# Running all six key chunks' scores of pairs 10 and 11 as one TensorE group

## The chip, the core and the metric

The kernel runs on one core of one Trainium2 chip. The core has a TensorE (PE: matmuls; PEld: the loading of its stationary operand), a VectorE (DVE), a ScalarE (ACT), a GpSimd (POOL) and a SyncE (SP), which run side by side and wait for one another by semaphores; DMA engines move data. The metric is device time in microseconds (us) for one execution; lower is better.

## What is computed

The reference joins a sparse attention and a mixture of experts. Cut to what matters:

```python
# attention: q, k, v are (4 batches, 8 heads, 768 tokens, 64)
k_sum = k.reshape(B, H, 24, 32, D).max(axis=3)      # one summary key for each 32 tokens
v_sum = v.reshape(B, H, 24, 32, D).mean(axis=3)
scores_l = scale * q @ k.T, kept where |i - j| < 16   # local band
scores_s = scale * q @ k_sum.T + log(32)             # summaries
a = softmax(concat(scores_l, scores_s)); attn = a @ concat(v, v_sum)
# experts: x is attn as (3072 tokens, 512)
P = sinkhorn(exp(x @ w_gate))                        # 8 rounds of row and column scaling
out = sum over e of P[:, e] * (relu(x @ w1[e]) @ w2[e])   # 8 experts, hidden size 1024
```

## The kernel before

**Pairs.** Attention is done for pairs of heads: 4 batches x 8 heads give 16 pairs, 0 to 15, four for each batch. A pair has two heads of 64 channels, which lie in partitions 0 to 63 and 64 to 127, and six chunks of 128 tokens. Pairs 0 to 3 are done in halves of three chunks by functions of their own (names ending in `_h`); pairs 4 to 15 go through `pair_start` and `pair_whole`.

**Steps of one pair (4 to 15).** Keys and queries come by GpSimd's DMA (`load_qk`, L284) and are transposed to kT and qT: for pairs below `BY_DMA` = 12 on TensorE (L303) with a copy out (L207), for 12 to 15 by DMA transposes on SyncE's queue (`tr_dma`, L330). VectorE takes the maximum over 32 keys (`key_max`, L335) and splits it by head (L341). TensorE multiplies keys and queries in the band, 64 rows by 128 columns (L347, tile sg). ScalarE exponentiates (`score_exp`, L408, tile er), VectorE multiplies by the band (`masks`, L412, tile em) and by the band's edges (`edges`, L420 and L424, tile Ee). TensorE multiplies queries by the summary keys (L461, tile ss), ScalarE exponentiates (L472). Values: block sums on TensorE (L357, tile vs), out by VectorE (L363, L367), the neighbours' values by small DMAs (`near_values`, L377 and L379; on SyncE's queue for pairs below 12, on GpSimd's from 12). TensorE multiplies by the values (L435, L441, tile av), VectorE normalizes (L542, L543, tile xs), and the result is transposed into xT, on TensorE (L550) with a copy or, for pairs 12 to 14, by DMA (L560).

**Halves or whole.** The scores of a pair need 2 heads x 6 chunks of 160 columns. A half (three chunks, both heads) fills the two PSUM banks of tag "s". For pairs below `WHOLE` the first half (`scores`) is exponentiated by one activation of 128x960; the second half (`scores_1`) takes the same two banks after that, and again one activation of 128x960. From `WHOLE` on, `scores` runs all six chunks in one go: the second half goes to two banks of tag "a", of which there are three, shared with transposes, block sums, summaries, values and logits, and is exponentiated by two activations of 128x480, one for each head.

**Experts.** Expert 0 (L211 to hidden tiles hps, L216 to outputs yps, in three banks of tag "m") runs on the tokens as they become ready, between the steps of attention. When a batch is ready its logits are taken (L570). Experts 1 to 7 follow (L764, L786, L798, L815, L830, L839, L843) with the Sinkhorn rounds (L579 to L593) among the first of them.

**Order.** The program isn't scheduled by the compiler. `Plan` (L34 to L125) is a list scheduler that runs while the kernel is built: each step is added with its engine (or a choice of ScalarE and VectorE), a cost, its dependencies, a priority and the PSUM buffers that it opens or uses; `order` picks the step that can start first and writes out one fixed order for each engine. Costs of the steps at hand: scores of a half 0.4, of a whole 0.6, exponentials 0.97 and 0.53 us. So an edit to one step can move many others, on every engine, and can change which of ScalarE and VectorE takes a step. Each engine then works through its order and waits where a semaphore isn't there yet. SyncE's transposes for a pair (L889) also wait for the scores of the pair three before.

Of the kernel before, what the change touches and what calls it, by code (L numbers as in the profile page):

```python
# [33 lines left out]
class Plan:  # L34
# [7 lines left out]
    def add(self, eng, cost, fn, deps=(), prio=0.0, opens=(), uses=(), lag=0.0):  # L42
        u = Unit(eng, cost, fn, [d for d in deps if d is not None], prio, list(opens), lag)
        for b in list(opens) + list(uses):
            b.users.append(u)
        if uses and eng != "PE":
            u.prio -= 100.0
        self.units.append(u)
        return u
# [79 lines left out]
def kernel(  # L129
# [29 lines left out]
    NEH = 3  # L159
    BY_DMA = 12  # L160
    X_BY_DMA = 12
    WHOLE = 12
    FILL = {"v0": 1, "S0": 1, "s0": 2, "s1": 1, "s2": 1}

    const = ctx.enter_context(tc.tile_pool(name="const", bufs=1))
# [60 lines left out]
    with tc.manual_schedule():  # L226
# [35 lines left out]
        def bank(tag, name, dtype=FP32):  # L262
            pool, n = (mps, 3) if tag == "m" else (aps, NA)
            return pool.tile([128, 2048 // mybir.dt.size(dtype)], dtype, tag=tag, name=name, bufs=n)
# [117 lines left out]
        def scores(i):  # L382
            sg = at["sg", i, 0] = banks2("sg")
            dst = [[sg[:, j, :] for j in range(2)], None]
            if i >= WHOLE:
                dst[1] = at["sg", i, 1] = [bank("a", "sg1") for _ in range(2)]
            score_mms(i, dst, range(G if i >= WHOLE else HG))

# [4 lines left out]
        def score_mms(i, dst, chunks):  # L393
            for g in chunks:
                for j in range(2):
                    o = (g % HG) * LIVE
                    score_mm(i, dst[g // HG][j][:, o:o + LIVE], j, g, 0, LIVE)

        def score_exp(i, h, j=None):
            if h == 0:  # L400
                at["er", i] = attn.tile([128, 2, G, LIVE], BF16, tag="er", name="er", bufs=2)
                at["em", i] = attn.tile([128, 2, G, 128], BF16, tag="em", name="em", bufs=2)
            er, sg = at["er", i][:, :, HG * h:HG * (h + 1), :], at["sg", i, h]
            if j is None:
                dst, src = er.rearrange("p j g l -> p j (g l)"), sg[:, :, 0:HG * LIVE]
            else:
                dst, src = er[:, j].rearrange("p g l -> p (g l)"), sg[j][:, 0:HG * LIVE]
            nc.scalar.activation(out=dst, in_=src, func=AF.Exp, bias=0.0, scale=SCALE)  # L408
# [535 lines left out]
        def pair_whole(i, prio):  # L944
# [3 lines left out]
            deps = [U["kT", i, 0], U["kT", i, 1], U.get(("ed", i - 2))]  # L948
            bufs = [Buffer("s")] + (2 * [None] if i < WHOLE else [Buffer("a"), Buffer("a")])
            U["S", i, 0] = U["S", i, 1] = add("PE", 0.4 if i < WHOLE else 0.6, lambda: scores(i), deps, prio,  # L950
                                              opens=[x for x in bufs if x is not None])
            U["X", i, 0] = add("ACT", 0.97, lambda: score_exp(i, 0), [U["S", i, 0]], prio, uses=bufs[:1])
            if i < WHOLE:
                buf = Buffer("s")
# [366 lines left out]
```

The softmax here doesn't subtract the row's maximum and nothing guards it: scores larger than these inputs give would overflow.

## Time and profile before

| | |
|---|---|
| median of 5 runs | 667.11 us (666.8 to 670.0) |
| the profiled execution | 668.27 us, its span 666.4 us |
| mean granted TensorE clock | 0.997 |
| TensorE busy | 658.5 us |
| first half of pair 10's scores starts at | 70.12 us |
| last score matmul (pair 15) starts at | 108.0 us |
| exponentials of scores | 20 of 128x960 and 8 of 128x480 |

A line of the timeline gives the start, the time from the first start to the last end, engine, line, operation, what is written and read, and how many in a row. Matmuls are pipelined and overlap, so the distance between starts tells what a group takes of TensorE. A line of waits gives engine and waiting line, who ended the wait, the sum of us, how many times, and the longest.

### The profile page before, as it was taken

Reading aid. Unit: us, or ns where it says so; the run is one execution under the profiler, and the core shown is the slowest. Engines: PE = TensorE matmul, PEld = TensorE weight load, DVE = VectorE, ACT = ScalarE, POOL = GpSimd, SP = SyncE. Lnnn points to the kernel's source line nnn. Section 1 sums busy time; section 2 is a strip of 40 time slices with the busy share of each in tenths; the row PEclk is TensorE's granted clock in tenths of the full one; section 3 lists DMA queues with packets and bytes.
Section 4 is the critical chain, followed back from the end, with each engine's and each line's share of the span. In section 5 each row is a group of like instructions: output and inputs, shape, how many; then the busy total and the mean of one; then the engine's idle time right before and its main releaser. Section 6 shows DMA issues by size and latency. Waiting matters only on the chain.

```text
span 666.4 us, 13247 instructions
## 1 busy us (share of the span) xinstructions
PE 658.5 (99%) x5132; PEld 436.7 (66%) x5132; DVE 550.3 (83%) x1034; ACT 411.9 (62%) x769; POOL 198.8 (30%) x257
## 2 busy tenths in 40 slices
PE   8999999999999999999999999999999999999997
PEld 4666666555676666666666666666666666666666
DVE  6899977798989787888789887888778877988776
ACT  5667876556876566556565665656565656556652
POOL 8899622100132222222221222222122213222123
PEclk8999999999999999999999999999999999999999
DMA  9999982700763747473654756373837465334656
GB/s 169 168 147 144 134 85 42 128 0 1 127 115 65 123 71 121 79 127 64 95 102 72 127 81 108 68 127 62 130 64 127 77 99 96 64 63 110 155 136 202
DMA packets 112558, 67.89 MB, mean 102 GB/s; under 512 B 77936, under 2 KB 90480, under 8 KB 112496
## 3 DMA queue, kind: packets, MB, share of 16 engines
q0 software_dynamic: 94816, 57.46, 65.1%
q1 hardware_dynamic: 17152, 9.58, 6.5%
q8 instruction: 40, 0.66, 0.4%
q14 instruction: 22, 0.18, 0.1%
q10 hardware_dynamic: 528, 0.02, 0.0%
HBM read 52.45 MB, written 6.29 MB: 88 GB/s over the span
## 4 chain that ended last, share of the span: by engine, by line
PE 96%; DVE 2%; DMA 1%; issue 0%; ACT 0%; POOLq 0%; DVEq 0%
PE yps L815 22%; PE pA L764 22%; PE pY L815 17%; PE pQ L764 11%; PE hps L211 6%; PE yps L216 6%; PE pR L764 5%; PE sg L347 1%; DMA qst<-in_q_dram 1%; PE av L512 1%; PE vs L357 1%; PE tkq L303 1%; PE av L435 1%; DVE xs L543 1%; PE ss L461 1%; PE av L441 1%
## 5 line engine op out<-in xcount | busy, mean ns | idle before, releaser
L815 PEld LDWEIGHTS <-h 128*128 128x128 f16 x2352 | 230.1, 98 | 89.2 <-issue 1.3
L843 POOL DMA_DIRECT2D out_acc<-y x120 | 101.4, 888 | 372.4 <-ACT y L839 106.4
L839 ACT ACTIVATE y<-pY,P_sb 128x256 f32<-128x256 f32 x168 | 80.0, 477 | 126.1 <-PE pY L815 124.6
L830 DVE SCALAR_TENSOR_TENSOR out_acc<-yps,P_sb,out_acc 128x512 f32<-128x512 f32 x128 | 95.1, 744 | 28.0 <-PE yps L815 27.9
L798 DVE TENSOR_TENSOR h<-h 128x1024 f16<-128x1024 f16 x168 | 109.1, 684 | 1.3
L815 PE MATMUL pY<-w,h 128*128 128x256 f16 x672 | 100.3, 273 | 0.6 <-ACT y L839 0.6
L764 PE MATMUL pA<-xT,w 128*128 128x512 f16 x336 | 98.6, 379 | 0.0
L815 PE MATMUL yps<-w2sum,h 128*128 128x256 f16 x672 | 97.9, 273 | 0.0
L815 PE MATMUL yps<-w,h 128*128 128x256 f16 x672 | 93.3, 273 | 0.0
L830 DVE SCALAR_TENSOR_TENSOR out_acc<-pY,P_sb,out_acc 128x512 f32<-128x512 f32 x84 | 62.8, 748 | 29.1 <-PE pY L815 27.6
L764 PEld LDWEIGHTS <-w 128*128 128x128 f16 x672 | 65.8, 98 | 31.3 <-issue 0.2
L764 PEld LDWEIGHTS <-w1sum 128*128 128x128 f16 x504 | 49.3, 98 | 44.7
L786 DVE CUSTOM_DVE_ANT_0 h<-pQ,snap 128x512 f16<-128x512 f32 x84 | 57.6, 686 | 6.5 <-ACT snap L207 3.6
L786 DVE CUSTOM_DVE_ANT_0 h<-pA,snap 128x512 f16<-128x512 f32 x84 | 57.3, 683 | 5.4 <-PE pA L764 5.1
L202 ACT ACTIVATE h<-pA 128x512 f16<-128x512 f32 x84 | 50.7, 603 | 12.1 <-PE pA L764 12.0
L202 ACT ACTIVATE h<-pR 128x512 f16<-128x512 f32 x84 | 50.1, 596 | 8.1 <-PE pR L764 8.1
L207 ACT COPY pR<-pA 128x512 f32<-128x512 f32 x82 | 46.8, 571 | 6.7 <-PE pA L764 5.9
L815 PE MATMUL pY<-w2sum,h 128*128 128x256 f16 x336 | 50.4, 273 | 0.1
L764 PE MATMUL pA<-xsum,w 128*128 128x512 f16 x168 | 50.0, 379 | 0.0
L764 PE MATMUL pQ<-xsum,w1sum 128*128 128x512 f16 x168 | 50.0, 379 | 0.0
L764 PE MATMUL pR<-xT,w 128*128 128x512 f16 x168 | 50.0, 379 | 0.0
L764 PE MATMUL pQ<-xT,w1sum 128*128 128x512 f16 x168 | 50.0, 379 | 0.0
(150 smaller groups left out, 856.7 us busy)
## 6 DMA issues: line engine op xcount, KB each, us to landing
out_acc<-y POOLq DMA_DIRECT2D x120, 256.0 KB, 3.4
w<-in_moe_w_dram POOLq DMA_DIRECT2D x14, 1024.0 KB, 10.3
out_dram<-out_acc SPq DMA_DIRECT2D x24, 256.0 KB, 2.4
qst<-in_q_dram POOLq DMA_DIRECT2D x32, 96.0 KB, 5.6
vx<-in_v_dram POOLq DMA_DIRECT2D x15, 192.0 KB, 6.4
kst<-in_k_dram POOLq DMA_DIRECT2D x24, 96.0 KB, 5.9
w<-in_moe_w_dram POOLq DMA_DIRECT2D x4, 256.0 KB, 8.0
w<-in_moe_w_dram POOLq DMA_DIRECT2D x2, 512.0 KB, 8.3
```

What stands on the lines that cost most here:

```text
L202: nc.scalar.activation(out=out, in_=in_, func=AF.Relu, bias=0.0, scale=1.0)
L207: (nc.scalar.copy if eng == "ACT" else nc.vector.tensor_copy)(out=out, in_=in_)
L211: nc.tensor.matmul(hp[:, 0:n], lhsT=w1s[e][:, dk, f * 128:(f + 1) * 128], rhs=xT[:, dk, t0:t0 + n], start=(dk == 0), stop=(dk == KD - 1))
L216: nc.tensor.matmul(yp[:, d], lhsT=h[:, f, c * 128:(c + 1) * 128], rhs=w2s[e][:, f, d], start=(f == 0), stop=(f == KF - 1))
L303: nc.tensor.transpose(t[:, g * 128:(g + 1) * 128], st[:, g, :, :].rearrange("p j d -> p (j d)"), ident)
L764: nc.tensor.matmul(dst[:], lhsT=lhsT, rhs=rhs, start=first and k == 0, stop=k == HK - 1, skip_group_check=True)
L786: nc.vector._custom_dve(dve_ops.TENSOR_ADD_SAT, out=ring(e, p, q)[:, q % 2, blk, :], in0=at[src, e, p, q][:], in1=at.pop(("snap", n, e, p, ...
L798: nc.vector.tensor_tensor(out=h[:, :, out_, :], in0=h[:, :, a, :], in1=h[:, :, b, :], op=op)
L815: nc.tensor.matmul(dst[:, d], lhsT=lhsT, rhs=rhs, start=f == 0 and n in (1, 5, 2), stop=f == HF - 1, skip_group_check=True)
L830: nc.vector.scalar_tensor_tensor(out=o, in0=y, scalar=scalar, in1=o, op0=ALU.mult, op1=ALU.add)
L839: nc.scalar.activation(out=at[key][:, d], in_=src, func=AF.Copy, bias=0.0, scale=P_sb[:, t, e:e + 1])
L843: nc.gpsimd.dma_start(out=o, in_=at.pop(("y", e, p, c, key))[:], accum_op=ALU.add)
```

## The change

One constant: `WHOLE` goes from 12 to 10. Pairs 10 and 11 then take the path of pairs 12 to 15 in `scores`, `score_exp` and `pair_whole`: one group of twelve score matmuls instead of two groups of six, the second half in two "a" banks, and its exponential in two activations. Since the order is planned anew, other steps move as well.

```diff
-    WHOLE = 12
+    WHOLE = 10
```

What it switches, unchanged in text:

```python
if i >= WHOLE:
    dst[1] = at["sg", i, 1] = [bank("a", "sg1") for _ in range(2)]
score_mms(i, dst, range(G if i >= WHOLE else HG))
...
bufs = [Buffer("s")] + (2 * [None] if i < WHOLE else [Buffer("a"), Buffer("a")])
...
if i < WHOLE:
    buf = Buffer("s")
    U["S", i, 1] = add("PE", 0.4, lambda: scores_1(i), deps, prio, opens=[buf])
    U["X", i, 1] = add("ACT", 0.97, lambda: score_exp(i, 1), [U["S", i, 1], U["X", i, 0]], prio,
                       uses=[buf])
else:
    x1 = [add("ACT", 0.53, lambda j=j: score_exp(i, 1, j), [U["S", i, 0], U["X", i, 0]], prio,
              uses=bufs[1 + j:2 + j]) for j in range(2)]
    U["X", i, 1] = x1[1]
```

## The prediction, made before the run

> **What bounds the kernel now.** I read the page's engine shares first, then TensorE's own waits, then the table of stretches for 60 to 120 us, then TensorE's timeline around the score groups, and last the landings of the key transposes.
>
> ```profile
> PE 658.5 (99%) x5132; PEld 436.7 (66%) x5132; DVE 550.3 (83%) x1034; ACT 411.9 (62%) x769; POOL 198.8 (30%) x257
> ...
> PE 96%; DVE 2%; DMA 1%; issue 0%; ACT 0%; POOLq 0%; DVEq 0%
> ```
>
> TensorE is busy 658.5 of 666.4 us, and the chain that ended last lies on it for 96%. Its waits, in full:
>
> ```profile
> PE idle L613 <- DVE zeros L632: 1.3, 1, 1.3
> PE tkq L312 <- DMA qst<-in_q_dram: 0.9, 1, 0.9
> PE pY L815 <- ACT y L839: 0.6, 1, 0.6
> PE tkq L300 <- ACT kst L207: 0.6, 1, 0.6
> ```
>
> None is in the stretch that the change touches: three are in the first microseconds, and the one at L815 is at the end. In that stretch TensorE is shown busy throughout (columns: TensorE, weight loads, VectorE, ScalarE, GpSimd, clock, DMA share, GB/s):
>
> ```profile
> 70.00:80.00 10.00, 10.00 (x123) 6.80 (x122) 9.62 (x27) 8.57 (x14) 6.86 (x8) 1.00 2.21 141
> 80.00:90.00 10.00, 10.00 (x96) 6.34 (x95) 9.23 (x26) 6.61 (x14) 2.17 (x4) 1.00 1.75 146
> 90.00:100.00 10.00, 10.00 (x109) 5.94 (x108) 6.39 (x18) 7.67 (x15) 2.10 (x4) 1.00 0.35 28
> ```
>
> The clock is 1.00 there. So time can go only by making TensorE's own sequence shorter, and can come only from a wait that doesn't exist now. Since a busy bar hides short waits, I use distances between starts in the timeline:
>
> ```profile
> 75.20 1.46 PE L211 MATMUL hps<-xT,w 128*128 128x384 f16 x8
> 76.60 0.38 PE L347 MATMUL sg<-qT,kT 64*128 64x160 bf16 x6
> 76.92 0.82 PE L211 MATMUL hps<-xT,w 128*128 128x384 f16 x4
> ...
> 89.59 1.46 PE L211 MATMUL hps<-xT,w 128*128 128x384 f16 x8
> 90.89 0.51 PE L357 MATMUL vs<-vx,m_blk 128*128 128x128 bf16 x6
> ...
> 94.54 0.59 PE L347 MATMUL sg<-qT,kT 64*128 64x160 bf16 x12
> 95.06 2.76 PE L216 MATMUL yps<-w,h 128*128 128x512 f16 x12
> ```
>
> A half (six matmuls) takes 76.92 - 76.60 = 0.32 us, a whole pair (twelve) 95.06 - 94.54 = 0.52. And entering a score group costs extra: the eight hidden matmuls ahead of it take 76.60 - 75.20 = 1.40, the same eight ahead of an ordinary group 90.89 - 89.59 = 1.30.
>
> **The change, part by part.** *Score groups.* For pairs 10 and 11 two groups of six become one of twelve; the number of matmuls is unchanged. Two halves: 2 x (0.10 + 0.32) = 0.84. One whole: 0.10 + 0.52 = 0.62. That is 0.2 us less for each pair, 0.4 for both, all on the path, as TensorE has no gap there. The Trainium skill has a rule for it: "TensorEngine Tiling (Array Packing)", Key Properties, says that a change of tiling mode drains TensorE. The row (64*128 for scores, 128*128 around them) agrees and gives the price, so I use the row.
>
> *The rule that speaks against it* is on the same page, Gotcha 1: PSUM Pressure: row tiling needs more PSUM banks, and different row tiles go to different ones. A half takes the two "s" banks. A whole takes these and two of the three "a" banks, through which block sums, summaries, values and transposes also pass. By the rule, each of the two pairs would make TensorE wait until two readers have let go. A bank is let go in about 0.54 + 0.80 us (the transposes of 91.23 to their copy's start at 91.77, and the copy), against some 1.2 us of other TensorE work that the order puts between: 0.1 to 0.2 us for each, 0.4 at most. By the row it costs 0: pairs 12 to 15 already take their banks so, at 94.54, 97.75, 103.00 and 107.60, and the groups ahead of them show only the 0.1 of entering. I take 0 and keep 0.4 for the range. What hides it is expert 0's matmuls, which use three banks of their own; were they used up, it would cost what it says.
>
> *Exponentials.* The second half's 128x960 activation (971 ns) becomes two of 128x480 (572 each): 0.17 us more ScalarE for a pair, 0.35 in all, on an engine busy 8.6 and 6.6 of 10 us here. Cover: TensorE's score-value products come several groups later. 0.
>
> *What moves.* The built program's order decides the rest, and I compared the two. TensorE's first difference is pair 10's first score group (70.12 in the trace); from what is at 205 us the sequences agree to the end, and VectorE's and ScalarE's agree from about 209. So experts 1 to 7 can't change by more than this stretch hands on. Inside it, expert 0's matmuls go ahead where halves stood; pair 10's scores move to behind pair 11's block sums, and by adding the measured groups that puts them near 81.8 instead of 70.1, pair 11's near 85.9 instead of 76.6. Pair 12 then comes some 2 us earlier and pairs 13 to 15 some 2 to 3 us later. VectorE gets two evacuations more on balance (pair 11's key and query copies go to it from ScalarE), about 0.55 us each; it is busy 9.6 of 10 before 80 us, and less so after it, where they fall. 0, with 0.2 for the range.
>
> *Small waits.* Between 180.37 and 182.44, eight L815 matmuls take 1.16 where others take 0.87, and four take 0.48 instead of 0.44: 0.33 us of wait on banks that ScalarE empties. The order around it is new. Bounds: gone (-0.33), or another such beside it (+0.3). I take -0.2, nearer to gone, since it is the only such place between 70 and 640 us.
>
> *SyncE's queue.* The four near-value transfers of pair 11 now stand ahead of pair 13's key and query transposes, and these, with those of pair 14, wait for the scores of pairs 10 and 11 (three pairs back). Behind the waiting transposes stand only later transposes. GpSimd's order is unchanged apart from when values free its near-value transfers; the weights of expert 1 are issued at 118.0 and needed at 129.16, 8.0 us to landing, so 3 us are to spare and about 1 us later does no harm. 0.
>
> *VectorE's queue.* This is the weak spot. Key maxima (952 ns) read keys transposed by DMA, and VectorE takes its work in order. Pair 12's maximum now stands ahead of pair 9's normalization, those of pairs 13 and 14 ahead of pair 11's, pair 15's ahead of pair 12's. If the keys have not landed, VectorE stands, and the values, the transposes to xT and TensorE behind them. The transfers to landing (kT alone):
>
> ```profile
> L330 SPq DMA_TRANSPOSE kT<-kst x4: 1217/1272/3037, 67.8 to 85.1; - x4
> ...
> DMA to landing us min/median/max: 7.0/7.6/8.7
> ```
>
> Pair 12: issued 67.84, landed 74.98; VectorE gets there after the maximum of pair 10 (75.47 before) plus 0.87 + 0.24: 76.6. Margin 1.6. Pair 13: issued about 82.5, wanted about 93.4 (row durations in the new order): 10.9 allowed, safe. Pair 14: issued after pair 11's scores, about 86.6; wanted about 94.6, so 8.0 allowed, against 7 to 8: margin about 0 to 1. Pair 15: issued about 93.3, wanted about 99.5, 6.2 allowed. The 7.0 to 8.7 belong to the time of heavy loads (141 and 146 GB/s); from 90 us on it is 28 GB/s, and the three xT transposes there took 2.7 to 3.6. I take 4 to 5, so it is in time. From both sides: nothing if so; at 8.7 for both, 0.7 + 2.5 of VectorE standing, less up to 0.6 of slack each ahead of TensorE, some 2 us. Below nothing is excluded, as no wait on these exists now.
>
> **Sum.** -0.4 (groups) - 0.2 (small waits) = -0.6. The profiled execution took 668.27 us for a span of 666.4; it would become 667.7 and 665.8. It was 1.16 above the median of the five runs, 667.11, which I carry the difference to: 666.5 us.
>
> **Rivals.** *Keys late (slower).* VectorE stands before the maxima of pairs 14 and 15 and TensorE after it. Point from which it decides: pair 14's keys over 8 us, or pair 15's over 6.2 + 0.6 us after issue; each microsecond past it is a microsecond. Likeliest case, 8.0 for pair 15: 1.8 - 0.3 of slack = +1.5, so -0.6 + 1.5 = +0.9: 668.0 us. At 8.7 for both 668.5, at the longest transposed landing seen (a query's, 9.8) about 670. For: four of four key transposes took 7.0 or more. Against: the quiet queues at that time. 17 in 100.
>
> *Bank starvation.* The rule's price twice, and again where the new order packs the wholes of 12 to 15 closer: 0.2 x 4 = 0.8, so +0.2: 667.3 us. For: two of three banks held for 4 us (pair 14's last exponential ends at 107.0). Against: four such pairs without a wait. 12 in 100.
>
> *It doesn't do what it says.* The halves' gain is real, but expert 0's matmuls that covered other waits are used up earlier, and a wait of the same size returns at the end of the batch: 667.1 us. Against: over 40 us of expert 0's work are left behind pair 15. 8 in 100.
>
> *Forecast*, 666.5: 63 in 100.
>
> **How the numbers follow.** Of five runs three lie within 0.3 of the median, the others 1.2 and 2.9 above it; so the forecast alone is 665.8 to 667.4. To hold 8 in 10, with banks and the nearer half of late keys, the range is 665.7 to 668.4. A measurement of this kernel tells about 0.3% from no change, 2.0 us: 665.1 and 669.1. Faster than that needs 1.4 us more than I find, as all the waits there are in the stretch come to about 0.5: 0.03. Slower needs late keys near the worst, or something not seen: 0.10. Within: 0.87.
>
> **What would show it.** Right: six groups of L347 x12 from pair 10 on, no x6 after 68 us; 0.52 us each; TensorE busy 10.00 in every stretch of ten; the first matmuls of expert 1's end at 205 come 0.4 to 0.7 us earlier. Keys late: VectorE idle before ks L335, released by a DMA, and TensorE idle at L550 or L357 near 95 to 105 us. Banks: TensorE waits at L347, L357 or L461, released by ScalarE or VectorE. I would be wrong in the whole if TensorE's groups cost more in their new neighbourhood, or the order after 209 us were to run with gaps.

## The result, and the profile after

| | before | after |
|---|---|---|
| median, us | 667.11 | 666.35 (665.96 to 669.54, 33 runs) |
| ratio to before | 1 | 0.9987, 95% interval 0.9981 to 0.9993 |
| profiled execution, its span, us | 668.27, 666.4 | 666.22, 664.3 |
| score groups of pairs 10 and 11 start at, us | 70.12 (the first half of pair 10) | 80.36 and 84.47 |

The kernel became 0.13% shorter, 0.87 us by the ratio (0.5 to 1.3 by its interval). That interval excludes "no difference", though the change is smaller than the 0.3% (2.0 us) that the prediction took as the least a measurement can tell. The median is 0.15 us from the forecast time. Times here and below are medians of executions at the full clock; one of e3, with 1145.54 us at a granted clock of 0.558, is left out. The page of after, TensorE's busy time and the chain that ended last:

```profile
PE 657.7 (99%) x5132; PEld 436.1 (66%) x5132; DVE 549.7 (83%) x1036; ACT 410.9 (62%) x769; POOL 199.0 (30%) x257
...
PE 95%; DVE 3%; DMA 1%; issue 0%; ACT 0%; SPq 0%; DVEq 0%
```

TensorE has the same 5132 matmuls and still is the chain. Its waits in after, in full, and then the three stretches of ten microseconds in which the change lies (columns as before):

```profile
PE idle L613 <- DVE zeros L632: 1.3, 1, 1.3
PE pY L815 <- ACT y L839: 0.6, 1, 0.6
```

```profile
70.00:80.00 10.00, 10.00 (x88) 6.25 (x86) 8.58 (x24) 5.48 (x11) 5.80 (x7) 1.00 2.13 140
80.00:90.00 10.00, 10.00 (x107) 6.52 (x106) 7.99 (x20) 7.63 (x15) 1.80 (x4) 1.00 1.34 142
90.00:100.00 10.00, 10.00 (x100) 5.81 (x99) 9.54 (x28) 8.14 (x15) 2.46 (x5) 1.00 0.11 19
```

No new wait shows: TensorE is busy throughout, at a clock of 1.00. What is gone from the waits are the two on the first loads (qst and kst, 0.9 and 0.6 us), and those belong to the start, where the two programs are alike. So the spans (2.1 us apart) can't be subtracted. I take distances between starts on TensorE instead:

| stretch, us | before | after | difference |
|---|---|---|---|
| start of the span to a common hidden matmul of expert 0, ahead of the change | 69.54 | 68.14 | -1.40 |
| from there to the first matmul of the common order of the end | 135.51 | 134.78 | -0.73 |
| from there to the end | 461.34 | 461.35 | 0.01 |

Only the -0.73 is the change's: up to the common matmul the two programs are the same. It is in two places. The first is the score groups, in TensorE's timeline of after:

```profile
80.36 0.59 PE L347 MATMUL sg<-qT,kT 64*128 64x160 bf16 x12
80.89 0.51 PE L303 MATMUL tkq<-ident,kst 128*128 128x128 bf16 x6
...
84.47 0.59 PE L347 MATMUL sg<-qT,kT 64*128 64x160 bf16 x12
85.00 1.47 PE L211 MATMUL hps<-xT,w 128*128 128x384 f16 x8
```

Both pairs have their twelve matmuls in one group, which takes 0.53 us (80.89 - 80.36 and 85.00 - 84.47). The second is near 180 us, where before had 0.33 us of short waits. First before, then after:

```profile
180.37 1.32 PE L815 MATMUL pY<-w2sum,h 128*128 128x256 f16 x8
181.53 0.60 PE L815 MATMUL pY<-w,h 128*128 128x256 f16 x4
```

```profile
179.44 1.04 PE L815 MATMUL pY<-w,h 128*128 128x256 f16 x8
180.32 0.60 PE L815 MATMUL yps<-w2sum,h 128*128 128x256 f16 x4
```

The order is another, so these are not the same matmuls, but eight of one shape: they take 181.53 - 180.37 = 1.16 us before and 180.32 - 179.44 = 0.88 after. The rest of the 0.33 is 0.04 in the four behind them. In exchange a wait of 0.03 us has come at 160.67. The sum is -0.42 (two switches fewer, at 0.21) - 0.33 + 0.03 = -0.72, against -0.73 measured.

### The profile page after: what moved, and what is told of

Same layout as the page of the kernel before. It is cut to its first block, busy times and chain, and to the rows that moved or that the text cites. A ratio compares the mean times of both kernels' runs of the same rounds, so it can differ in the third digit from the quotient of the medians.

```text
span 664.3 us, 13258 instructions
## 1 busy us (share of the span) xinstructions
PE 657.7 (99%) x5132; PEld 436.1 (66%) x5132; DVE 549.7 (83%) x1036; ACT 410.9 (62%) x769; POOL 199.0 (30%) x257
## 4 chain that ended last, share of the span: by engine, by line
PE 95%; DVE 3%; DMA 1%; issue 0%; ACT 0%; SPq 0%; DVEq 0%
PE yps L815 22%; PE pA L764 22%; PE pY L815 17%; PE pQ L764 11%; PE hps L211 6%; PE yps L216 6%; PE pR L764 5%; PE sg L347 1%; DMA kvf<-in_v_dram 1%; PE vs L357 1%; PE av L512 1%; PE tkq L303 1%; PE av L435 1%; DVE xs L543 1%; PE ss L461 1%; PE av L441 1%
## 5 line engine op out<-in xcount | busy, mean ns | idle before, releaser
L764 PE MATMUL pA<-xT,w 128*128 128x512 f16 x336 | 98.3, 379 | 0.0
L815 PE MATMUL yps<-w,h 128*128 128x256 f16 x672 | 93.3, 273 | 0.0
L764 PEld LDWEIGHTS <-w 128*128 128x128 f16 x672 | 65.8, 98 | 31.6 <-issue 0.2
L764 PEld LDWEIGHTS <-w1sum 128*128 128x128 f16 x504 | 49.3, 98 | 45.0
L764 PE MATMUL pA<-xsum,w 128*128 128x512 f16 x168 | 50.0, 379 | 0.0
L764 PE MATMUL pQ<-xsum,w1sum 128*128 128x512 f16 x168 | 50.0, 379 | 0.0
L764 PE MATMUL pA<-xsum,w1sum 128*128 128x512 f16 x168 | 50.0, 379 | 0.0
L764 PE MATMUL pQ<-xT,w1sum 128*128 128x512 f16 x168 | 50.0, 379 | 0.0
```

The source lines that it names most:

```text
L764: nc.tensor.matmul(dst[:], lhsT=lhsT, rhs=rhs, start=first and k == 0, stop=k == HK - 1, skip_group_check=True)
L815: nc.tensor.matmul(dst[:, d], lhsT=lhsT, rhs=rhs, start=f == 0 and n in (1, 5, 2), stop=f == HF - 1, skip_group_check=True)
```

## The experiments

Theory: each further score group costs TensorE about 0.2 us because the matmuls go from 128 rows to 64 and back; the rest of the difference is the order that the planner happens to write. Rivals: any interruption of a group costs as much; the wholes of pairs 10 to 15 gain less than they take in banks; keys come late. Differences of a few tenths of a microsecond are smaller than the intervals of the times (0.4 us each way at best). So each kernel has, beside its time, the distance on TensorE from the first score matmul of pair 4 to the end, in its one profiled execution: 631.00 us before, 630.28 after. Each ratio is to executions of the kernel before beside it (median 666.95 us beside e1 to e4, 666.84 beside e5 to e8); it is not the quotient of the medians.

**A switch put back in (e1), an interruption without a switch (e2).** Both are after, with one small matmul between the halves of the twelve of pairs 10 to 15, written to a place that the next matmul overwrites. It has 128 rows in e1 and 64, as the scores have, in e2.

```diff
+    if g == HG and len(chunks) == G:
+        nc.tensor.matmul(dst[1][0][:, 0:64], lhsT=zeros[0:128, 0:128], rhs=zeros[0:128, 0:64],
+                         start=True, stop=True)        # e2: zeros[0:64, ...]
```

> The changed kernel with one matmul of 128 rows and 64 columns on zeros put between the two halves of the twelve-matmul score groups of pairs 10 to 15; it writes a bank that the next score matmul overwrites. TensorE's order is otherwise that of the changed kernel, and the results are the same. Theory of the mode switch: each of the six groups leaves the 64-row mode and enters it again, about 0.16 + 0.10 us, less the 0.07 between two score matmuls that was there, and 0.03 for the matmul, so about 0.2 us each and 1.2 to 1.4 in all over the changed kernel: some 0.4 to 0.6 us above the kernel before. Rival, that the gain came from the new order alone: six times 0.03 = 0.2 us over the changed kernel, still faster than before by 0.5.

> The same with the zero matmul in 64 rows, the mode of the scores, so that nothing switches. Theory of the mode switch: a seventh matmul in each half-group costs what two score matmuls cost apart, 0.03 to 0.07 us, so 0.2 to 0.4 us over the changed kernel and about 1 us less than the run with 128 rows. Rival of an interruption as such (any foreign matmul costs a pipeline's length): the same time as with 128 rows.

e1 took 667.74 us (ratio to before 1.0016, 1.0008 to 1.0024), e2 666.26 (0.9995, 0.9985 to 1.0006). The distances are 631.88 and 630.44, so +1.60 and +0.16 over after. TensorE's timelines, e1 and then e2, with the weight load of the inserted matmul:

```profile
80.58 0.38 PE L347 MATMUL sg<-qT,kT 64*128 64x160 bf16 x6
80.89 0.10 PEld L396 LDWEIGHTS <-zeros 128*128 128x128 bf16 x1
80.90 0.20 PE L396 MATMUL sg<-zeros 128*128 128x64 bf16 x1
81.03 0.38 PE L347 MATMUL sg<-qT,kT 64*128 64x160 bf16 x6
```

```profile
80.19 0.38 PE L347 MATMUL sg<-qT,kT 64*128 64x160 bf16 x6
80.34 0.09 PEld L396 LDWEIGHTS <-zeros 64*128 64x128 bf16 x1
80.40 0.19 PE L396 MATMUL sg<-zeros 64*128 64x64 bf16 x1
80.41 0.39 PE L347 MATMUL sg<-qT,kT 64*128 64x160 bf16 x6
```

From the first six to the second six it is 0.45 us in e1 and 0.22 in e2. With 128 rows, 0.11 more passes on leaving (0.32 against 0.21) and 0.12 more on coming back (0.13 against 0.01). The two kernels differ in nothing but those rows. Behind the second six 0.01 is given back, so that each of the six places costs 0.22 us and all of them 1.30. The distances differ by 1.44 and the medians by 1.48; the 0.15 left of the distances is a single wait in e1, at L818 near 555 us. This shows that it is the switch, and not the interruption, that costs. The weight load itself is no longer with 128 rows (0.10 us against 0.09), but it starts later: with its matmul in e1 (80.89 and 80.90), 0.06 us ahead of it in e2.

**Halves for more pairs (e3: all; e5: pairs below 14).** `WHOLE` = 16 and 14.

```diff
-    WHOLE = 10
+    WHOLE = 16        # e5: 14
```

> WHOLE = 16: all pairs from 4 on in two halves. Theory of the mode switch: four pairs more in halves than before, 4 x 0.2 = +0.8 us over the kernel before, 1.2 plus or minus small waits over the changed one. Rival, that wholes cost by the banks which they hold and the gain was luck of the order: no slower than before, or faster.

> WHOLE = 14: pairs 12 and 13 in halves too, 14 and 15 whole. Theory of the mode switch: two groups more than before, +0.4 us on the stretch from pair 4's first score matmul to expert 1's common order, plus or minus the small waits that the new order has (the kernel before has 0.33 near 180 us). Rival, bank starvation already in the kernel before: at or under the time of before.

e3 took 668.2 us (1.0023, 1.0014 to 1.0032), e5 667.69 (1.0004, 0.9991 to 1.0016, which alone decides nothing). The distances are 632.41 and 631.57. For every kernel I counted the score groups from pair 4 on, and the waits of the stretch, short ones inside busy bars too (a start later than the group's own step allows). Those near the end, from 645 us on, are the same 1.02 us in every kernel and are left out:

| kernel | groups | distance, us | waits, us | distance without waits |
|---|---|---|---|---|
| e4, whole from 8 | 16 | 632.51 | 2.91 | 629.60 |
| after, whole from 10 | 18 | 630.28 | 0.31 | 629.97 |
| before, whole from 12 | 20 | 631.00 | 0.61 | 630.39 |
| e7, as before, other order | 20 | 631.41 | 1.03 | 630.38 |
| e5, whole from 14 | 22 | 631.57 | 0.75 | 630.82 |
| e3, halves for all | 24 | 632.41 | 1.18 | 631.23 |

The last column rises by 0.19 to 0.22 us for each group, over all six kernels. What the times add to that are the waits. The largest of e3 in its timeline:

```profile
91.74 0.35 PE L435 MATMUL av<-vx,em 128*128 128x65 bf16 x6
92.75 0.40 PE L441 MATMUL av<-Ve,Ee 128*128 128x130 bf16 x3 [0.67 <-DVE h L204]
```

Six L435 take 0.18 us elsewhere and 1.01 here, so 0.83 of wait. The VectorE step that is named as releaser has nothing to do with these values: the neighbours' values of this pair (12) were issued from 83.24 on, and the last landed at 92.62. e5 has a wait of 0.39 at the same place, put down to that transfer. Neither wait was in what I expected.

**Wholes for more pairs (e4: from 8; e8: from 4).**

```diff
-    WHOLE = 10
+    WHOLE = 8         # e8: 4
```

> WHOLE = 8: pairs 8 and 9 whole as well. Theory of the mode switch alone: another -0.4 us, so about 1.1 us under the kernel before. Rival, bank starvation: pairs 8 and 9 still have their keys and queries transposed on TensorE through the three banks that a whole takes two of, and less work of expert 0 is ready there; each whole then makes TensorE wait for 0.5 to 1 us at a time, ahead of L461 and L550 between 65 and 85 us, and once more near 100 us: some 2 to 3 us in all, so 2 us slower than before.

> WHOLE = 4: all pairs from 4 on whole. Groups alone: six pairs more than in the changed kernel, -1.2 us. Bank starvation: pairs 4 to 8 run while expert 0 has little ready, and each whole makes TensorE wait 1 to 3 us for values, transposes and summaries: 5 to 8 us slower than before in all.

e4 took 668.68 us (1.0033, 1.002 to 1.0045): two groups fewer than after, and 2.6 us more of waits. e8 took 675.2 (1.0116, 1.0092 to 1.0141). Here the price that was named for the banks exists, but in e4 it is the smaller part. e4's waits that after doesn't have (line, who ended it, sum, times, longest):

```profile
PE tx L550 <- DVE xs L543: 0.8, 3, 0.3
...
PE ss L461 <- DVE ksT L341: 0.5, 1, 0.5
PE av L435 <- ACT xT L207: 0.4, 1, 0.4
```

Only the last is a bank that a reader (the copy to xT) lets go. The first two are TensorE waiting for results of VectorE, mostly at 62.99 to 64.53 us. By distances between starts they come to 1.9 us and the bank to 0.4; another 0.4 at 100.44, not on the page, follows neighbours' values that landed at 100.32. In after two half groups stand in that place (62.88 and 64.86) and give VectorE the time. Fewer pieces of TensorE work to put between, as much as banks, make wholes dear there; how much of it the planner's count of banks causes through its order was not separated. In e8 a wait for a bank is plain. It lies in a stretch of TensorE's timeline, from 56 to 69 us, in which no expert's matmul stands between the steps of attention any more:

```profile
62.85 0.50 PE L461 MATMUL ss<-qT,ksT 128*128 128x384 bf16 x2 [0.46 <-DVE ksT L341]
64.44 0.49 PE L303 MATMUL tkq<-ident,qst 128*128 128x128 bf16 x6 [1.08 <-ACT Ee L472]
```

Transposes of queries read nothing that the exponential Ee writes; the bank is the only tie between them. After these waits the granted clock falls (the column behind GpSimd's):

```profile
50.00:60.00 10.00, 8.96 (x92) 5.23 (x90) 8.04 (x20) 7.29 (x13) 10.00 (x13) 1.00 2.25 142
60.00:70.00 10.00, 7.30 (x88) 5.17 (x88) 9.34 (x28) 6.26 (x11) 9.46 (x13) 0.83 2.28 141
```

The largest waits on e8's list come later: 2.5 us in three, at 163 to 181 us, where L764 waits for copies by ScalarE. How these follow from the change was not followed up.

**Late keys on purpose (e6).** After, with the key transpose of pair 15 done five times over (the same result each time), so that it lands late.

```diff
-            nc.sync.dma_start_transpose(...)
+            for _ in range(5 if (i, z) == (NP - 1, 0) else 1):
+                nc.sync.dma_start_transpose(...)
```

> The changed kernel with pair 15's key transpose issued five times, each waiting for the one before; the results are the same. One takes some 3 us to landing there, so the last lands about 101 to 103 us instead of 89.0, and VectorE wants it at 98.15. Theory of late keys: VectorE stands 3 to 5 us ahead of L335, TensorE some tenths less than that at the values and transposes behind it (L550, L435, L461), and the kernel is 2.5 to 4.5 us slower than the changed one. Rival, that VectorE has enough work in hand elsewhere: no more than 0.5 us.

It took 672.9 us (1.0082, 1.0054 to 1.011), 6.6 over after in the distance: more than I had expected. The chain is the one that was described. VectorE's and TensorE's timelines and then four stretches of e6 (a line added makes L335 and L461 L336 and L462):

```profile
103.73 0.95 DVE L336 TENSOR_REDUCE ks<-kT 128x24 bf16<-128x768 bf16 x1 [5.62 <-DMA kT<-kst]
...
105.69 0.82 PE L462 MATMUL ss<-qT,ksT 128*128 128x384 bf16 x2 [4.54 <-DVE xs L544]
```

```profile
100.00:105.00 5.00, 1.15 (x14) 0.71 (x12) 1.24 (x3) 0.77 (x2) 2.07 (x4) 0.83 0.74 90
105.00:108.00 3.00, 2.31 (x12) 1.46 (x13) 2.90 (x9) 0.97 (x2) 0.00 (x0) 0.50 0.00 0
108.00:111.00 3.00, 3.00 (x44) 1.73 (x43) 1.68 (x6) 1.37 (x4) 0.00 (x0) 0.65 0.36 68
111.00:116.00 5.00, 5.00 (x49) 3.02 (x49) 4.26 (x12) 3.07 (x6) 2.07 (x4) 1.00 0.08 14
```

VectorE stood 5.62 us for the keys. TensorE stood 4.70 behind it by the distance between starts (the page shows 4.54), so 0.9 us were slack. The missing 1.9 us come between 105.69 and 110.23, in the stretches of the next two lines: the granted clock is 0.50 and 0.65 while TensorE works again, and a step of 384 columns takes 0.32 us instead of 0.16. So a microsecond of late keys is not "a microsecond", as the prediction had it, once the wait is this long.

**The order alone (e7).** Before, with the cost by which the planner plans a half's scores changed from 0.40 to 0.41. No step is added or removed; only the order written differs.

```diff
-    add("PE", 0.4, lambda: scores_1(i), ...)
+    add("PE", 0.41, lambda: scores_1(i), ...)     # and the first half alike
```

> The kernel before with one number of the planner changed: the cost of a half's scores is 0.41 instead of 0.40 us. The program has the same instructions and the same structure (halves for pairs 4 to 11); only the order is another. Theory of the mode switch with small waits: the groups cost the same, and what differs is waits: pairs 10 to 13 values waiting for near values or edges, 1 to 3 us slower than before. Rival, that the order is of no account and only the number of groups matters: the same as before within 0.3 us.

It took 667.71 us (1.0002, 0.9989 to 1.0016): no difference that this interval tells, where I had expected 1 to 3. The distance is 0.41 longer than before's. Its groups cost the same; its waits are others:

```profile
87.11 0.35 PE L435 MATMUL av<-vx,em 128*128 128x65 bf16 x6
87.58 0.34 PE L441 MATMUL av<-Ve,Ee 128*128 128x130 bf16 x3
...
181.18 0.60 PE L815 MATMUL pY<-w,h 128*128 128x256 f16 x4
182.01 0.59 PE L764 MATMUL pQ<-xT,w1sum 128*128 128x512 f16 x2 [0.24 <-ACT snap L207]
```

By distances between starts they are 0.29 us at 87.58 (again neighbours' values, landed at 87.45) and 0.40 at 182.01. So the order alone moved this kernel's profiled execution by some 0.4 us, as much as the two switches.

No kernel run here beats the changed one.

## Why the prediction was right, point by point

- **Score groups, -0.4:** right. Measured -0.42, and e1 against e2 show the cause, which until then was a rule of the Trainium skill ("TensorEngine Tiling (Array Packing)", Key Properties: a change of mode drains TensorE) and a row that agreed with it. The 0.10 in the sum was entering alone; about as much for leaving was hidden in the 0.32 and 0.52 of the groups, so the sum came out right.
- **Banks, 0:** right for pairs 10 and 11. Neither group waits, nor do those of 12 to 15. The rule set against the change ("TensorEngine Tiling (Array Packing)", Gotcha 1: PSUM Pressure) is not empty: with wholes from pair 4 on, a bank's reader holds TensorE up for 1.08 us at one place. What was named as the cover, expert 0's matmuls, fits: they stand beside pairs 10 and 11, and at that place of e8 they were missing. No run took away the cover alone, so that it is the cover which separates the two is argued and not shown.
- **Exponentials and moves, 0:** right; ScalarE and VectorE are busy 5.5 to 9.5 of 10 us in the three stretches, and TensorE waits for neither. Pair 10's scores were put near 81.8 and pair 11's near 85.9 on before's clock; they are at 81.8 and 85.9, when 1.40 is added for the earlier start.
- **Small waits, -0.2:** the sign right, the size 0.1 short: -0.33 near 180 us, +0.03 elsewhere. The -0.2 was chosen between two bounds, and that the waits went was luck as far as can be told: it came with the new order, and e7, with before's steps in yet another order, has 0.40 there. Why this order has none is not shown.
- **SyncE's queue, 0:** right in the sum, wrong in the reason. I had the key transposes of pairs 13 and 14 wait for the scores of the pair three before, and the description of the kernel above says the same. That is how the planner orders them; the program written waits only for the readers of the transpose's buffer, which the pair four before had used. In after both were issued ahead of the scores named, which started at 80.36 (pair 10) and 84.47 (pair 11):

```profile
78.67 2.13 SPq L330 DMA_TRANSPOSE kT<-kst  x1
...
82.35 2.42 SPq L330 DMA_TRANSPOSE kT<-kst  x1
```

- **VectorE's queue, 0, "the weak spot":** it was none, for the later pairs. Pair 14's transpose was issued at 82.35, which is 83.75 on before's clock (I had reckoned about 86.6), and pair 15's at 86.29, or 87.69 (93.3). They landed at 86.81 and 89.03 and were read at 93.14 and 98.15: margins of 6.3 and 9.1 us, where I had 0 to 1 and 1 to 2. Pair 12's margin was the small one, landed at 73.80 and read at 75.24, 1.4 us against 1.6 reckoned. With such margins 17 in 100 for late keys was too much, and e6 shows that their price was too low: 6.6 us for 5.6 of standing, where a microsecond was to be a microsecond less some slack.
- **The sum, -0.6:** -0.73 in the trace and -0.87 (0.5 to 1.3) in the times. The 0.1 between sum and trace is the term of the small waits. The point common to both orders came 0.73 us earlier, just past the 0.4 to 0.7 that was named.
- **Rivals:** none happened. "It doesn't do what it says" would need the gain to be given back later, and the last 461 us are the same within 0.01.

## What to carry to other kernels

Where TensorE is the bound, count how often neighbouring matmuls change their number of rows and price the change from distances between starts in the timeline; putting groups of like shape together paid here while other matmuls stood between the steps, which cover what the larger group holds. Before expecting a gain of some tenths of a microsecond from such an edit in a planned order, plan once with a cost changed slightly: how far that moves the waits says how much of a result is the edit's. For what an instruction waits, look at the semaphores in the program written, not at the dependencies that the planner was given.

## What the runs showed of the hardware that was not expected

- At a change of rows TensorE's weight load doesn't run ahead. In after, from pair 4 on, the first load of a group starts 0.004 to 0.005 us before its matmul at all 35 changes between 128 and 64 rows; where one group of 128 rows follows another, the first load is 0.02 us or more ahead in 112 of 113 cases up to 112 us (median 0.06). That fits a drain at each change; how much of the 0.1 us of each side is the load is not shown.
- A wait of 4.7 us on TensorE (e6) cost 1.9 us more through the clock, which was at 0.50 when work began again at 105.69 and back at 1.00 by 111. The Trainium skill, "TensorE: Matmul & The Clock Gate", Part 1, has the clock halved after an idle window of about 3.4 us and freed after about as much work. The trace agrees in the half and, within a microsecond, in the recovery: by the mean of 0.65 from 108 to 111 it ended near 110.1, after 4.4 us of work (an estimate). It doesn't agree in the start: by the mean of 0.83 from 100 to 105 the clock fell near 103.3, some 2.3 us into the wait (an estimate too). In e8 the clock fell though no wait of that stretch was over 1.1 us; TensorE was busy 7.30 of the ten microseconds, and the mean was 0.83.
- A busy bar hid waits of up to 0.3 us: of the 0.61 us of waits that distances between starts give for before in that stretch, and the 0.31 for after, the page shows none. Longer ones are shown some 0.16 us short (0.67 for 0.83 in e3, 0.24 for 0.40 in e7, 4.54 for 4.70 in e6).
- An engine named as releaser can be a bystander: in e3 the wait at 92.75 is put down to VectorE, and the transfer that it needed had landed 0.13 us ahead of it.
